# Transposed loads issued a stage earlier, and two elementwise passes moved to GpSimd with their neighbour sums moved to ScalarE

## The chip, the cores and the metric

The kernel runs on one core of one Trainium2 chip. The time is the device time of one execution in microseconds (us), given as the median over executions. Engines are named as in the profile: PE is TensorE, DVE is VectorE, ACT is ScalarE, POOL is GpSimd, SP is the engine whose queue issues nearly all DMAs here.

A ratio between two kernels is the mean time of one kernel's fast runs over the mean of the other's fast runs in the same rounds on the same chip, with a 95% interval. So it is not quite the ratio of the medians that stand beside it.

## The reference, cut to what matters

The forward pass is a modulated layer norm, a spectral mixing of the 2048 x 512 tokens (2-D FFT, product with complex weights, inverse FFT), a second modulated layer norm, and a two-layer network with squared ReLU. The kernel computes the output and the gradients of all nine differentiable inputs.

```python
x = A_x
mod = (silu(c) @ w_mod).reshape(1, 6, 1, 512)      # sa, ca, ga, sb, cb, gb
h = layernorm(x) * (1 + ca) + sa
x = x + ga * irfft2(rfft2(h) * (w_r + 1j * w_i))
h = layernorm(x) * (1 + cb) + sb
x = x + gb * (relu(h @ w1 + b1) ** 2 @ w2 + b2)
# reference: (x, *vjp(x wrt A_x, w_r, w_i, w1, b1, w2, b2, c, w_mod)(grad_out))
```

What this study touches is the last third of the backward pass:

- the **w1 stage**: the second spectral pass over eight groups of columns, which gives the gradients of w_r and w_i (tile gW), interleaved with the gradient of w1 (tile gw in its line 1085 before, 1086 after) and the gradient of w_mod (tiles wmc, gm_junk, gwm);
- the **short spectral stage** (tiles psG, utcs), whose first product marks the end of the w1 stage;
- the **last phase**: eight pairs of 128-row blocks go through the inverse transform and the backward of the first layer norm, while TensorE fills its time with the gradient of w2 (tile gw of line 1153 before, 1156 after). Column sums over the rows (tile acc) give two modulation gradients at the end.

## The kernel before

The loads of h for the w2 gradient are transposing DMAs of 512 KB into four rotating tiles. Before, the first four are issued behind the stage that needs the space, together with the first rows:

```python
    spec_f23(tc, K, UT, AEs, None, ..., ew_b, after_b)    # the w1 stage; after_b(gi) runs after each group
    lf2.release()
    gwp = tc.alloc_tile_pool(name="gwp", bufs=1, side="right")
    g_sb = gwp.tile([P, NT, D], BF16, name="g_sb")
    hns, endp = [], {}

    def load_hn():
        fc = len(hns)
        if fc < NFC:
            hns.append(endp.get("hn", gwp).tile([P, NT, P], BF16, name="hn", bufs=4))
            nc.sync.dma_start(hns[fc], h_dram[fc, :, :], transpose=True)
    # ... grad_w2, load_rows3 (two row loads per pair, n1 and gxl, from the same queue) cut ...
    nc.sync.dma_start(g_sb, g_view)
    load_hn()
    load_rows3(0)
    load_rows3(2)
    for _ in range(3):
        load_hn()
```

What runs after each group of the w1 stage, and two users of the same DMA queue in it:

```python
        def after_b(gi):
            if gi + 4 < 8:
                load(gi + 4)                  # Z, Xb and constants of a later group
            if gi == 4:
                nc.sync.dma_start(K["LG"], LG_dram)
            fill_w1(2 if 0 < gi < 6 else 1)   # w1 units: 16 matmuls, a copy on ScalarE, an output DMA
            if gi % 2 == 1:
                gms.pop(0)()                  # one w_mod gradient: GMod.emit
    # grad_w1: the output tile of two units
        if fb % 2 == 0:
            w1o[0] = gwa.tile([P, 2, W4], BF16, name="gw1", bufs=2)
        nc.scalar.copy(out=w1o[0][:, fb % 2, :], in_=ps[:, 0:W4])
        if fb % 2 == 1:
            nc.sync.dma_start(out4_view[...], w1o[0]...)
    # GMod.emit
            wmc = pool.tile([P, 2, D], BF16, name="wmc", bufs=self.bufs)      # bufs 2 here
            nc.sync.dma_start(wmc, self.wm_view[:, dc:dc + 2, cs])
            # ... on VectorE: sum of wmc * gmbc into junk ("gm_junk", line 465); gwm goes out by DMA ...
```

The row work of one pair in the last phase (gh1 is unfolded from gs by four 512-element passes on VectorE, lines 261 to 265):

```python
            nc.vector.tensor_tensor(gn, gh1, modb[...], op=ALU.mult)                                # line 1228
            for i in range(2):
                nc.scalar.activation(gs[:, i, :], gn[:, i, :], AF.Copy, scale=..., accum_out=rr[:, i, 0:1])
            nc.vector.tensor_tensor(q1, gh1, n1, op=ALU.mult)
            late.add(lambda: colsums1(t, gh1, q1))                                                  # TensorE
            for i in range(2):
                jk = fp.tile([P, D], BF16, name="jk1", bufs=1)
                nc.vector.scalar_tensor_tensor(out=jk, in0=gs[:, i, :], scalar=K["onef"], in1=n1[:, i, :], op0=ALU.mult, op1=ALU.mult,
                                               accum_out=rr[:, i, 1:2])
            nc.vector.tensor_scalar(rr[:, :, 2:4], rr[:, :, 0:2], -1.0 / D, None, op0=ALU.mult)
            for i in range(2):
                nc.vector.tensor_scalar(gn[:, i, :], n1[:, i, :], rr[:, i, 3:4], rr[:, i, 2:3], op0=ALU.mult, op1=ALU.add)
            nc.vector.tensor_tensor(gs, gn, gs, op=ALU.add)
            gx = fp.tile([P, 2, D], BF16, name="gx")
            nc.vector.tensor_tensor(gx, gs, gxl, op=ALU.add)
            nc.sync.dma_start(out1_view[:, t:t + 2, :], gx)
            load_rows3(t + 4)
```

## Time and profile before

| | us |
|---|---|
| median of 3 runs | 434.45 (434.1 to 438.83) |
| the profiled execution | 438.28, of which the trace covers 436.5 |
| first product of the short spectral stage (the w1 stage's end) | 340.8 |
| first and last pass q of the row chain | 362.9, 418.2 |
| last column sum | 419.1 |

The last three rows are starts in the trace, counted from its beginning. The profiled execution is the slow end of the three, so I use a second trace of the same kernel beside it (the last experiment), where the marks are 338.1, 359.9, 414.4, 415.3 and the end 432.7.

The stages and the waits of this trace stand in the prediction. Two lines more will be needed as a yardstick, the groups of two VectorE passes of the row chain between 345 and 437 us (after the bar: total busy us, mean ns of one; then the idle time before them):

```profile
L1228 DVE TENSOR_TENSOR gn<-gh,modb 128x1024 bf16<-128x1024 bf16 x8 | 5.5, 688 | 0.1
L1239 DVE TENSOR_SCALAR gn<-n,rr 128x512 bf16<-128x512 bf16 x16 | 5.8, 407 | 0.0
```

A pass over 1024 elements with two inputs takes 688 ns and one over 512 with per-partition scalars 407 ns, all of them nearly alike.

### The profile page before, as it was taken

To read this page: it belongs to the slowest core of one execution; us is meant where nothing else is said; L and a number is where in the kernel's file an instruction comes from. 1 tells how busy PE (TensorE), PEld (TensorE's weight loads), DVE (VectorE), ACT (ScalarE), POOL (GpSimd) and SP (SyncE) were. 2 spreads that over 40 slices of the span, in tenths; PEclk is the share of its full clock that TensorE was granted. 3 is DMA by queue.
4 is the path that set the end of the run, shared out by engine and by line. 5 is a ranking of instruction groups with operands and counts; after the bars stand their busy time and mean duration, and the time that the engine had idled before them with its cause. 6 is when DMAs were issued, how large, how long until landed. Compare 5 with 4: busy or idle time off the path is not lost.

```text
span 436.5 us, 7027 instructions
## 1 busy us (share of the span) xinstructions
PE 398.5 (91%) x2353; PEld 195.4 (45%) x2375; DVE 351.4 (80%) x846; ACT 261.2 (60%) x493; POOL 13.0 (3%) x64
## 2 busy tenths in 40 slices
PE   2789989999999999999999999999899799993996
PEld 0335446654444434443444444455455464441332
DVE  6887758959997588969897998909686968978896
ACT  5797889769881286348536765365348375445331
POOL 6120000000000000000000000000000000000000
PEclk9998999999999999999999999999999999999899
DMA  8995779999298469669965997987995699999984
GB/s 240 238 291 146 188 290 267 279 311 256 91 379 245 136 114 352 165 165 229 270 195 153 222 338 267 211 204 229 273 300 158 168 253 259 222 260 244 275 235 144
DMA packets 149738, 101.09 MB, mean 232 GB/s; under 512 B 98753, under 2 KB 135494, under 8 KB 149062
## 3 DMA queue, kind: packets, MB, share of 16 engines
q1 hardware_dynamic: 149138, 100.12, 86.6%
q10 hardware_dynamic: 564, 0.53, 0.4%
q8 instruction: 18, 0.29, 0.3%
q14 instruction: 18, 0.15, 0.1%
HBM read 35.44 MB, written 41.60 MB: 176 GB/s over the span
## 4 chain that ended last, share of the span: by engine, by line
PE 35%; DVE 28%; DMA 14%; ACT 12%; SPq 5%; issue 5%; POOL 1%; ACTq 0%; DVEq 0%
PE og L880 10%; PE mm L853 6%; PE mm L694 4%; PE mm L1150 4%; DMA n<-n_dram 3%; DMA out_dram<-gw 2%; DMA x<-in_A_x_dram 2%; DVE gm_junk L465 2%; PE psG L341 2%; SPq L1145 2%; PE mod_ps L595 2%; PE mm L1081 2%; DMA n_dram<-x_sb 2%; DVE l_st L795 1%; ACT r L855 1%
## 5 line engine op out<-in xcount | busy, mean ns | idle before, releaser
L694 PE MATMUL mm<-gT,w2T 128*128 128x512 bf16 x224 | 58.1, 383 | 3.4 <-DVE gab L697 2.7
L853 PE MATMUL mm<-h2T,w 128*128 128x512 bf16 x224 | 53.6, 379 | 1.7 <-ACT r L855 1.5
L1150 PE MATMUL mm<-g_sb,hn 128*128 128x512 bf16 x217 | 51.6, 387 | 3.8 <-DVE gw L1153 3.4
L1081 PE MATMUL mm<-gab,h_sb 128*128 128x448 bf16 x256 | 51.5, 352 | 2.5 <-ACT gw L1085 2.5
L880 PE MATMUL og<-w1T,gab 128*128 128x512 bf16 x218 | 49.9, 379 | 1.1 <-DVE o L945 0.8
L880 PE MATMUL og<-w,h 128*128 128x512 bf16 x217 | 49.1, 379 | 0.3
L855 ACT ACTIVATE r<-mm,b1col 128x512 bf16<-128x512 f32 x56 | 37.0, 684 | 6.1 <-PE mm L853 3.7
L1081 PEld LDWEIGHTS <-h_sb 128*128 128x128 bf16 x256 | 24.6, 98 | 24.2 <-issue 3.6
L853 PEld LDWEIGHTS <-w 128*128 128x128 bf16 x224 | 21.1, 97 | 30.6 <-issue 8.8
L1150 PEld LDWEIGHTS <-hn 128*128 128x128 bf16 x224 | 21.3, 99 | 29.8 <-issue 7.1
L880 PEld LDWEIGHTS <-h 128*128 128x128 bf16 x224 | 21.8, 98 | 26.1 <-issue 0.9
L880 PEld LDWEIGHTS <-gab 128*128 128x128 bf16 x224 | 21.6, 98 | 25.9 <-issue 1.4
L694 PEld LDWEIGHTS <-w2T 128*128 128x128 bf16 x224 | 20.9, 98 | 23.1 <-issue 6.5
L893 ACT CAST G<-og 128x512 bf16<-128x512 f32 x16 | 9.2, 580 | 27.9 <-PE og L880 27.9
L699 ACT CAST gab<-mm 128x512 bf16<-128x512 f32 x36 | 21.7, 602 | 3.0 <-PE mm L694 2.9
L857 DVE TENSOR_TENSOR h<-r 128x1024 bf16<-128x1024 bf16 x28 | 19.2, 687 | 4.8 <-ACT r L855 4.8
L1085 ACT CAST gw<-mm 128x448 bf16<-128x448 f32 x16 | 8.7, 543 | 24.0 <-DMA out_dram<-gw 15.0
L1230 ACT ACTIVATE gs<-gn,inv 128x512 bf16<-128x512 bf16 x16 | 11.4, 716 | 18.3 <-DVE gn L1228 18.3
L413 DVE TENSOR_TENSOR p<-Z,G 128x1028 bf16<-128x1028 bf16 x8 | 5.6, 697 | 19.9 <-DMA Xb<-xs_dram 11.6
L372 ACT ACTIVATE Tsb<-psT 128x512 bf16<-128x512 f32 x32 | 18.5, 604 | 1.6 <-PE psT L370 1.6
L465 DVE SCALAR_TENSOR_TENSOR gm_junk<-wmc,onef,gmbc 128x512 bf16<-128x512 bf16 x24 | 17.9, 747 | 1.9 <-DMA wmc<-in_w_mod_dram 1.0
L697 DVE CAST gab<-mm 128x512 bf16<-128x512 f32 x20 | 13.7, 686 | 6.8 <-PE mm L694 6.7
(287 smaller groups left out, 757.1 us busy)
## 6 DMA issues: line engine op xcount, KB each, us to landing
h_dram<-h SPq DMA_DIRECT2D x28, 256.0 KB, 3.6
gh_dram<-gab SPq DMA_DIRECT2D x28, 256.0 KB, 3.8
w<-in_B_w_dram SPq DMA_DIRECT2D x2, 1792.0 KB, 7.7
wmc<-in_w_mod_dram SPq DMA_DIRECT2D x12, 256.0 KB, 4.7
out_dram<-gwm SPq DMA_DIRECT2D x12, 256.0 KB, 3.7
wz_dram<-Z SPq DMA_DIRECT2D x8, 258.0 KB, 2.4
xs_dram<-Xs SPq DMA_DIRECT2D x8, 258.0 KB, 3.2
Z<-wz_dram SPq DMA_DIRECT2D x8, 258.0 KB, 4.3
```

Source lines behind the costliest of these rows:

```text
L372: nc.scalar.activation(Tsb, ps, AF.Copy, scale=EF_S)
L465: nc.vector.scalar_tensor_tensor(out=junk, in0=wmc[:, i, :], scalar=K["onef"], in1=gmbc, op0=ALU.mult, op1=ALU.mult, accum_out=self.gsc[:, ...
L694: nc.tensor.matmul(ps, lhsT=w2T[:, dc, fc * P:(fc + 1) * P], rhs=gT[b][:, :, dc, :], start=(dc == 0), stop=(dc == 3))
L697: nc.vector.tensor_copy(out=gaT[b][:, fc, :], in_=ps)
L699: nc.scalar.copy(out=gaT[b][:, fc, :], in_=ps)
L853: nc.tensor.matmul(ps, lhsT=w1[:, dc, (fc + i) * P:(fc + i + 1) * P], rhs=h2T[b][:, :, dc, :], start=(dc == 0), stop=(dc == 3))
L855: nc.scalar.activation(r[:, i, :], ps, AF.Relu, bias=b1col[:, fc + i:fc + i + 1])
L857: nc.vector.tensor_tensor(h2, r, r, op=ALU.mult)
L880: nc.tensor.matmul(ps, lhsT=lhs(fc), rhs=rhs[:, fc, :], start=(fc == 0), stop=(fc == NFC - 1))
L1081: nc.tensor.matmul(ps[:, 0:W4], lhsT=h2_sb[:, t, dc * P:(dc + 1) * P], rhs=ghn[t // 4][:, t % 4, fs], start=(t == 0), stop=(t == NT - 1))
L1150: nc.tensor.matmul(ps, lhsT=hns[fc][:, t, :], rhs=g_sb[:, t, :], start=(t == 0), stop=(t == NT - 1))
L1230: nc.scalar.activation(gs[:, i, :], gn[:, i, :], AF.Copy, scale=inv1[:, t + i:t + i + 1], accum_out=rr[:, i, 0:1])
```

## The change

Its intent: the transposed loads should leave the crowded start of the last phase, and VectorE should lose four of its costliest passes per pair to engines that have time, GpSimd (q and gx) and ScalarE (the running sums, with a new product on VectorE in front of them).

```diff
+    hnp = tc.alloc_tile_pool(name="hnp", bufs=1, side="right")      # ahead of the w1 stage
+    hns, endp = [], {}
+    def load_hn(): ...                                              # as before, with hnp in place of gwp
@@ after_b(gi)
                 nc.sync.dma_start(K["LG"], LG_dram)
+            if 1 <= gi < 5:
+                load_hn()
             fill_w1(2 if 0 < gi < 6 else 1)
@@
     nc.sync.dma_start(g_sb, g_view)
-    load_hn()
     load_rows3(0)
     load_rows3(2)
-    for _ in range(3):
-        load_hn()
@@ row_pair
-            nc.vector.tensor_tensor(q1, gh1, n1, op=ALU.mult)
+            nc.gpsimd.tensor_tensor(q1, gh1, n1, op=ALU.mult)
             late.add(lambda: colsums1(t, gh1, q1))
+            nc.vector.tensor_tensor(gn, gs, n1, op=ALU.mult)
             for i in range(2):
-                jk = ...; nc.vector.scalar_tensor_tensor(out=jk, ..., accum_out=rr[:, i, 1:2])
+                nc.scalar.activation(gn[:, i, :], gn[:, i, :], AF.Copy, accum_out=rr[:, i, 1:2])
@@
-            nc.vector.tensor_tensor(gx, gs, gxl, op=ALU.add)
+            nc.gpsimd.tensor_tensor(gx, gs, gxl, op=ALU.add)
```

I call the first half part 1 and the edits in row_pair part 2.

More of the change, by code (lines that the diff above doesn't have):

```diff
@@ L1087, in grad_w1, with load_hn @@
             nc.sync.dma_start(out4_view[:, dc, (fb - 1) * W4:(fb + 1) * W4], w1o[0].rearrange("p a f -> p (a f)"))
+    hns, endp = [], {}
+    def load_hn():
+        fc = len(hns)
+        if fc < NFC:
+            hns.append(endp.get("hn", hnp).tile([P, NT, P], BF16, name="hn", bufs=4))
+            nc.sync.dma_start(hns[fc], h_dram[fc, :, :], transpose=True)
     units = []
@@ L1137 @@
     g_sb = gwp.tile([P, NT, D], BF16, name="g_sb")
-    hns, endp = [], {}
-    def load_hn():
-        fc = len(hns)
-        if fc < NFC:
-            hns.append(endp.get("hn", gwp).tile([P, NT, P], BF16, name="hn", bufs=4))
-            nc.sync.dma_start(hns[fc], h_dram[fc, :, :], transpose=True)
     def grad_w2(fc):
@@ L1230, in row_pair @@
                 nc.scalar.activation(gs[:, i, :], gn[:, i, :], AF.Copy, scale=inv1[:, t + i:t + i + 1], accum_out=rr[:, i, 0:1])
-            nc.vector.tensor_tensor(q1, gh1, n1, op=ALU.mult)
+            nc.gpsimd.tensor_tensor(q1, gh1, n1, op=ALU.mult)
             late.add(lambda: colsums1(t, gh1, q1))
+            nc.vector.tensor_tensor(gn, gs, n1, op=ALU.mult)
             for i in range(2):
-                jk = fp.tile([P, D], BF16, name="jk1", bufs=1)
-                nc.vector.scalar_tensor_tensor(out=jk, in0=gs[:, i, :], scalar=K["onef"], in1=n1[:, i, :], op0=ALU.mult, op1=ALU.mult,
-                                               accum_out=rr[:, i, 1:2])
+                nc.scalar.activation(gn[:, i, :], gn[:, i, :], AF.Copy, accum_out=rr[:, i, 1:2])
             nc.vector.tensor_scalar(rr[:, :, 2:4], rr[:, :, 0:2], -1.0 / D, None, op0=ALU.mult)
@@ L1284 @@
     gwp.release()
+    hnp.release()
     h2p.release()
```

## The prediction

> **What bounds the kernel now.** I began with the page's table of busy time and then asked for the busy time of each engine by stage, because a share over the whole span mixes stages. The change only touches what happens after about 300 us: the second spectral pass with the w1 gradient (about 286 to 341 us), the short spectral stage after it (341 to 356), and the last phase, in which pairs of rows go through VectorE and ScalarE while TensorE works off the w2 gradient (356 to the end).
>
> ```profile
> PE 398.5 (91%) x2353; PEld 195.4 (45%) x2375; DVE 351.4 (80%) x846; ACT 261.2 (60%) x493; POOL 13.0 (3%) x64
> ```
> ```profile
> core 0: us, PE busy (x) PEld busy (x) DVE busy (x) ACT busy (x) POOL busy (x), PEclk, DMA share, GB/s
> 303.00:323.00 20.00, 18.28 (x115) 10.22 (x113) 14.73 (x38) 8.65 (x17) 0.00 (x0) 1.00 0.93 264
> 323.00:341.00 18.00, 17.19 (x111) 9.81 (x110) 13.85 (x32) 9.46 (x18) 0.00 (x0) 1.00 0.68 206
> 341.00:356.00 15.00, 12.60 (x120) 8.83 (x119) 14.52 (x35) 7.97 (x15) 0.00 (x0) 1.00 0.67 212
> 356.00:394.00 38.00, 37.48 (x232) 17.96 (x235) 29.44 (x71) 19.58 (x45) 0.00 (x0) 1.00 1.08 245
> 394.00:404.00 10.00, 3.12 (x21) 1.10 (x19) 8.62 (x21) 5.74 (x13) 0.00 (x0) 0.96 1.06 230
> 404.00:421.00 17.00, 16.89 (x76) 6.43 (x77) 15.73 (x39) 5.53 (x13) 0.00 (x0) 0.92 1.00 257
> 421.00:433.00 12.00, 11.45 (x51) 4.63 (x50) 10.87 (x31) 3.84 (x6) 0.00 (x0) 1.00 0.70 217
> ```
>
> Read the PE column against the length of each stretch. TensorE is full nearly everywhere; what it loses is 1.72 + 0.81 us in the w1 gradient, 2.4 us in 341 to 356, 0.52 us, then 6.88 us in one hole from 394 to 404, then 0.11 and 0.55. The last column but one says that the DMA engines are full from 356 to 421. VectorE is busy but not full in any stretch except 341 to 356. So I asked for the chain of work around the hole, and for the DMA queue in the same time.
>
> ```profile
> 388.23 0.45 DVE gw L1153
> 388.68 3.98 DMA n<-n_dram
> ...
> 395.17 0.68 DVE gw L1153
> ...
> 397.83 3.95 DMA n<-n_dram
> 401.84 0.57 issue
> 402.41 0.70 DVE gw L1153
> 403.11 0.04 issue
> 403.15 1.86 PE mm L1150 x4
> ```
> ```profile
> 383.73 4.86 SPq L1145 DMA_TRANSPOSE hn<-h_dram  x2
> 388.68 0.53 SPq L1170 DMA_DIRECT2D n<-n_dram  x1
> ...
> 393.27 4.46 SPq L1145 DMA_TRANSPOSE hn<-h_dram  x1
> 397.83 0.52 SPq L1170 DMA_DIRECT2D n<-n_dram  x1
> ```
>
> The hole is a chain of four: a transposed load of h occupies the one DMA queue for 4 to 5 us; the row load n behind it is issued late and lands 4 us later; VectorE, which works in order, stands at its product q with n (the waits give 6.2 us in 3 waits for it, the first one at 362.9 us); and behind that product stands the eviction gw, which TensorE needs in order to reuse one of two PSUM tiles. Two such waits make the hole of 6.88 us. The bound of the last phase is thus the DMA queue, through VectorE's order, and TensorE's own work right behind it.
>
> **What the Trainium skill says.** "GPSIMD Engine Reference", section 3.1: a two-input elementwise pass costs about 2.6 cycles an element at 1.2 GHz, and VectorE is about twice as fast in fp32. The trace before has no pass of that size on GpSimd (its only tensor_tensor are 128x4 and took 1064 ns), so it neither agrees nor disagrees. "SBUF — State Buffer", section Who interferes with whom: a VectorE instruction with two SBUF inputs contends with a GpSimd instruction that reads SBUF, and the second one to issue can be blocked until the first is done. No stretch of this trace has both, so nothing shows it. "ScalarE: Activation LUTs", rules for kernel authors: about 0.3 us for an ACTIVATE and 0.83 ns an element, so 0.72 us for 512; the trace agrees (716 ns for the scaled copy with a sum, and 189 ns for reading the sum out). "DMA: Bandwidth & Descriptors", Latency and other measured facts: 261 GB/s for a transposing DMA, which makes 2.0 us for a tile of 512 KB; here the 14 loads of h held the queue for 3.1 us at the median (1.9 to 7.2), and landed in 5.6 us, so this case is slower, and I use its own number.
>
> **Part 1, the four early loads.** Four of the 14 transposed loads (2 MB) leave the stretch 351 to 370 us, where they take 7.23 us (the first, just behind the 2 MB load of the output gradient) and 8.52 us (the next three) of the queue, 15.7 us together. They come after groups 1 to 4 of the spectral pass, which I place at about 303 to 325 us. What this saves: the first n lands at 362.9 now, 11.6 us after the queue began the first transpose; without that transpose n is behind the gradient alone, so I expect it at about 358 to 360, and the first wait of 1.7 us disappears. The output and row loads from 361 on no longer stand behind 8.5 us of transposes. And the DMA engines, full for 58 us (14.7 MB between 351 and 409 us, 254 GB/s), have 2 MB less to move: 8.3 us at that rate, more than the 6.2 us that VectorE waits for n. I take it that the hole of 6.9 us closes: minus 6.9 us. More than that is not to be had, as TensorE is otherwise full from 356 on.
>
> What it costs: the w1 gradient stage. There the queue already works almost without a pause from 299 to 331 us, the DMA share is 0.93 from 303 to 323, and TensorE's 2.53 us of idle time come from one thing:
>
> ```profile
> ACT gw L1085 <- DMA out_dram<-gw: 15.0, 2, 8.0
> ```
>
> ScalarE cannot evict a w1 tile until the output of an older one has left, since there are two output tiles. Four more transposes of 3.1 us put 12.5 us into the queue in front of these outputs. Some of it is hidden: the queue waits for VectorE's gW for 6.8 us in that stage, TensorE has a lag of two tiles, and from 331 to 341 the queue has air. By estimate each of the two waits grows by a little over 1 us, plus 2.5 us in all, with 0 and 6 us as the bounds I can argue for.
>
> **Part 2, work taken from VectorE.** Start to start, a pass of 1024 elements with two inputs takes 0.60 us on VectorE in the timeline, one of 512 in the unfolding 0.34, one with a per-partition scalar 0.33, and the multiply with a running sum 0.67 and 0.08 for the read-out.
>
> ```profile
> L1235 DVE SCALAR_TENSOR_TENSOR jk<-gs,onef,n 128x512 bf16<-128x512 bf16 x16 | 12.0, 747 | 0.7 <-ACT gs L1230 0.3
> L1231 DVE TENSOR_TENSOR q<-gh,n 128x1024 bf16<-128x1024 bf16 x8 | 5.5, 687 | 6.2 <-DMA n<-n_dram 6.2
> L1242 DVE TENSOR_TENSOR gx<-gs,gxl 128x1024 bf16<-128x1024 bf16 x8 | 5.5, 683 | 0.0
> ```
>
> Each of the eight pairs of rows loses q (0.60), two sums (1.50) and gx (0.60) on VectorE and gains one product (0.60): minus 2.1 us a pair, minus 16.8 us over the phase. ScalarE gains two copies with a sum, 0.72 us each start to start, so 1.44 us a pair and 11.5 us in all; it is busy for about half of the phase now and stays under TensorE. GpSimd gets two passes of 1024 elements a pair: 1024 x 2.6 / 1.2 GHz = 2.2 us each by the skill's figure, 35 us over eight pairs, an estimate.
>
> What of this lies on the path: pairs of rows follow each other at 7.9 us now (q of the first pair at 362.94, of the last at 418.18, seven intervals), of which VectorE works about 7. The last pair's column sum releases the two modulation gradients, and from there to the end are some 17 us. TensorE's w2 gradient ends at the same time, 432.5 us. So a faster row chain alone cannot move the end, and a much slower one would.
>
> **The rivals.** First, the port: what VectorE keeps of a pair is nearly all with two SBUF inputs or in a fast mode: 4 x 0.34 + 3 x 0.60 + 2 x 0.33 = 3.8 us. If GpSimd and VectorE exclude each other wholly, a pair needs 3.8 + 4.4 = 8.2 us in place of 7.9, the saving of 16.8 us is paid back, and the row chain ends at about 360 + 7 x 8.2 = 418, as late as now. Then nothing comes from part 1 either, the cost in the w1 stage stays, and the time is 436 to 440. For it: the skill's rule. Against it: nothing in the trace; and GpSimd has more than half of the time free, so that part can fall beside evictions from PSUM. If both share the port by access, a pair takes about 7 us and the chain ends at about 410: then TensorE alone bounds the end. Second, the latency: the ring of two gs tiles already makes ScalarE wait for gx (12.3 us in 3 waits, the longest 5.4). The loop grows by ScalarE's sums and by GpSimd's 2.2 us in place of 0.60, from about 9 to 11 or 13 us for two pairs in flight, 5.5 to 6.5 us a pair; still under 7.9, so it is not the bound, but it uses up most of what VectorE gave. Third, the early loads may be hidden wholly in the w1 stage (the queue has waits of its own): then the time falls by 7 to 8 us, to 427. Fourth, they may make TensorE wait for both output tiles at each of the four loads: plus 6 us, and the time stays at 434.
>
> **Range and chances.** 434.45 - 6.9 (the hole) + 2.5 (the w1 stage) + 0.5 (the row chain's own spill under contention) = 430.5 us. The best case is TensorE's own floor: all of its idle time after 356, 6.88 + 0.52 + 0.11 + 0.55 = 8.1 us, gone at no cost, 426.4, which is still short of 2% (425.8). Only a gain in 341 to 356 as well, or in the w1 stage, would pass it. The worst that I can argue, the port exclusive and the w1 stage 6 us longer, is 440 to 445. So the range is 424.5 to 440, and the chances are 0.16 for faster by over 2%, 0.73 for within 2%, 0.11 for slower.
>
> **What would show it.** Right: TensorE's idle time between 356 and 433 falls from 8.1 us to 2 or less; VectorE no longer waits for n; the idle time of ScalarE for w1 outputs grows from 15 us; in the w1 stage TensorE loses some 5 us in place of 2.5; GpSimd's passes take 2.2 us or more, and VectorE's two-input passes become longer than 687 ns on average. Wrong: if a hole as long as the old one stands later in the last phase, with waits for GpSimd or ScalarE's sum (the ring or the port is the bound); if the passes on GpSimd last 4 us, so that it becomes the slowest engine of the row chain; or if the w1 stage ends as early as before (the early loads are free).

## The result, and the profile after

| | before | after |
|---|---|---|
| median us | 435.54 of 4 runs (434.1 to 438.83) | 461.10 of 4 runs (460.68 to 462.53) |
| ratio of the fast runs | | 1.0581 (95%: 1.0512 to 1.0651) |
| traced span | 436.5 | 459.0 |
| first product of the short stage | 340.8 | 354.9 |
| first and last q | 362.9, 418.2 | 375.1, 432.4 |
| last column sum | 419.1 | 434.9 |

The changed kernel is 5.8% slower and computes the same, correct outputs. The marks say at once that there are two losses: 14.1 us until the short stage starts, and a row chain that is no faster and leaves 24.1 us of work after its last column sum, where 17.4 were left before.

First the same stretches as in the prediction, for the kernel after (columns: stretch and its length, busy us and number of instructions of PE, PEld, DVE, ACT, POOL, the granted TensorE clock, the DMA engines' busy share, GB/s):

```profile
303.00:323.00 20.00, 16.08 (x92) 8.60 (x91) 10.63 (x26) 6.55 (x13) 0.00 (x0) 0.91 0.94 236
323.00:341.00 18.00, 15.56 (x99) 8.82 (x98) 10.95 (x26) 5.15 (x11) 0.00 (x0) 1.00 0.64 203
341.00:356.00 15.00, 8.11 (x35) 4.26 (x35) 7.10 (x18) 6.78 (x13) 0.00 (x0) 0.66 0.74 200
394.00:404.00 10.00, 6.21 (x30) 2.84 (x31) 7.75 (x13) 7.84 (x20) 5.72 (x3) 0.83 0.57 171
404.00:421.00 17.00, 12.51 (x77) 5.12 (x77) 15.57 (x24) 8.30 (x20) 9.44 (x5) 0.92 0.78 186
```

In the first two stretches TensorE now idles 3.9 and 2.4 us where it lost 1.7 and 0.8, and in the third, which is still the w1 stage here, 6.9 of 15 us. It also does less in its busy time: 92 products in 16.08 us against 115 in 18.28, at a granted clock of 0.91. The DMA engines have a third of their time free in the second of them and a quarter in the third (0.64 and 0.74), so throughput is not what all three engines lack there; something makes everybody wait in turn. In the last two stretches the old hole has company: TensorE idles 3.8 and 4.5 us, with the DMA engines at 0.57 and 0.78.

**The w1 stage.** The DMA queue, then the three engines at the worst place, from the timelines of the kernel after (start us, duration, and in brackets how long the engine stood before it and for what):

```profile
335.61 2.50 SPq L1132 DMA_DIRECT2D out_dram<-gW  x4
338.15 3.31 SPq L1096 DMA_TRANSPOSE hn<-h_dram  x1
341.57 0.52 SPq L1088 DMA_DIRECT2D out_dram<-gw  x1
...
345.41 0.44 SPq L458 DMA_DIRECT2D wmc<-in_w_mod_dram  x1
```
```profile
344.43 0.53 ACT L1086 CAST gw<-mm 128x448 bf16<-128x448 f32 x1 [9.13 <-DMA out_dram<-gw]
```
```profile
347.89 1.88 PE L306 MATMUL psC<-AE,LFb 128*128 128x257 bf16 x8 [9.33 <-ACT G L308]
```
```profile
348.90 0.75 DVE L465 SCALAR_TENSOR_TENSOR gm_junk<-wmc,onef,gmbc 128x512 bf16<-128x512 bf16 x1 [8.69 <-DMA wmc<-in_w_mod_dram]
```

Read it as a ring. Between 328.65 and 335.61 the queue issues nothing: its next entry is the output of gW, which VectorE has not made, because VectorE stood for 5.2 us at the product gm_junk, until the wmc tile had come at 330.57, and does the products of gm_junk before those of gW. Then come the gW outputs (2.5 us), a transposed load (3.3 us), and only then the w1 output for which ScalarE has stood 9.1 us, and the wmc tile for which VectorE has stood 8.7 us again. TensorE stands 9.3 us because the copies of G are behind ScalarE's blocked eviction. Before, the waits for wmc were 1.0 us in all and those for w1 outputs 15.0 us; after, they are 13.9 and 28.4.

**The last phase.** The groups of VectorE from 340 us to the end, then of GpSimd, in the kernel after:

```profile
L1238 DVE TENSOR_SCALAR gn<-n,rr 128x512 bf16<-128x512 bf16 x16 | 9.5, 633 | 0.2
...
L1228 DVE TENSOR_TENSOR gn<-gh,modb 128x1024 bf16<-128x1024 bf16 x8 | 9.0, 1129 | 0.1
L1156 DVE TENSOR_TENSOR gw<-mm,modb 128x512 bf16<-128x512 f32 x14 | 9.6, 683 | 2.3 <-PE mm L1153 2.3
```
```profile
L1231 POOL TENSOR_TENSOR q<-gh,n 128x1024 bf16<-128x1024 bf16 x8 | 19.7, 2458 | 133.3 <-PE psT L370 123.0 <-DVE gh L265 4.6 <-DVE rr L1236 2.5
L1241 POOL TENSOR_TENSOR gx<-gs,gxl 128x1024 bf16<-128x1024 bf16 x8 | 18.1, 2259 | 21.1 <-DVE gs L1239 19.0 <-issue 2.1
```

The two yardstick groups went from 407 to 633 ns and from 688 to 1129 ns, while the eviction gw, with one input in PSUM and one in SBUF, stays at 683. On the page, VectorE's busy time rose from 351.4 to 357.7 us, although the change took 16.8 us of passes from it by the prediction's count. A mean of 1129 ns hides what happens; a single place in the two timelines shows it:

```profile
378.95 0.68 DVE L1233 TENSOR_TENSOR gn<-gs,n 128x1024 bf16<-128x1024 bf16 x1
379.56 2.61 DVE L1228 TENSOR_TENSOR gn<-gh,modb 128x1024 bf16<-128x1024 bf16 x1
382.19 0.69 DVE L1156 TENSOR_TENSOR gw<-mm,modb 128x512 bf16<-128x512 f32 x1
```
```profile
379.17 2.45 POOL L1231 TENSOR_TENSOR q<-gh,n 128x1024 bf16<-128x1024 bf16 x1 [1.54 <-DVE gh L265]
```

The product that began before q takes its usual 0.68 us. The next one starts 0.4 us into q and lasts until 382.17: q's end (381.62) plus 0.55 us. It stood still for as long as GpSimd ran. Behind it, in order, stands gw, which TensorE needs. That gw itself is not held is visible at 392.95 us, where one takes 0.68 us in the midst of a q that runs from 392.39 to 395.0:

```profile
392.95 0.68 DVE L1156 TENSOR_TENSOR gw<-mm,modb 128x512 bf16<-128x512 f32 x1
```

### The profile page after: what moved, and what is told of

Same layout as the page of the kernel before. It is cut to its first block, busy times and chain, and to the rows that moved or that the text cites. A ratio compares the mean times of both kernels' runs of the same rounds, so it can differ in the third digit from the quotient of the medians.

```text
span 459.0 us, 7066 instructions
## 1 busy us (share of the span) xinstructions
PE 405.7 (88%) x2353; PEld 197.7 (43%) x2375; DVE 357.7 (78%) x806; ACT 271.8 (59%) x525; POOL 50.7 (11%) x80
## 5 line engine op out<-in xcount | busy, mean ns | idle before, releaser
L1082 PE MATMUL mm<-gab,h_sb 128*128 128x448 bf16 x256 | 55.0, 370 | 3.9 <-ACT gw L1086 3.9
L1082 PEld LDWEIGHTS <-h_sb 128*128 128x128 bf16 x256 | 25.7, 102 | 28.2 <-issue 9.3
L1231 POOL TENSOR_TENSOR q<-gh,n 128x1024 bf16<-128x1024 bf16 x8 | 19.7, 2458 | 133.3 <-PE psT L370 123.0
L853 PEld LDWEIGHTS <-w 128*128 128x128 bf16 x224 | 21.1, 97 | 30.6 <-issue 8.8
L1086 ACT CAST gw<-mm 128x448 bf16<-128x448 f32 x16 | 8.8, 549 | 40.7 <-DMA out_dram<-gw 28.4
L880 PEld LDWEIGHTS <-gab 128*128 128x128 bf16 x224 | 21.6, 98 | 25.9 <-issue 1.4
L465 DVE SCALAR_TENSOR_TENSOR gm_junk<-wmc,onef,gmbc 128x512 bf16<-128x512 bf16 x24 | 19.7, 822 | 14.7 <-DMA wmc<-in_w_mod_dram 13.9
L1241 POOL TENSOR_TENSOR gx<-gs,gxl 128x1024 bf16<-128x1024 bf16 x8 | 18.1, 2259 | 21.1 <-DVE gs L1239 19.0
```

Source lines behind the costliest of these rows:

```text
L465: nc.vector.scalar_tensor_tensor(out=junk, in0=wmc[:, i, :], scalar=K["onef"], in1=gmbc, op0=ALU.mult, op1=ALU.mult, accum_out=self.gsc[:, ...
L853: nc.tensor.matmul(ps, lhsT=w1[:, dc, (fc + i) * P:(fc + i + 1) * P], rhs=h2T[b][:, :, dc, :], start=(dc == 0), stop=(dc == 3))
L880: nc.tensor.matmul(ps, lhsT=lhs(fc), rhs=rhs[:, fc, :], start=(fc == 0), stop=(fc == NFC - 1))
L1082: nc.tensor.matmul(ps[:, 0:W4], lhsT=h2_sb[:, t, dc * P:(dc + 1) * P], rhs=ghn[t // 4][:, t % 4, fs], start=(t == 0), stop=(t == NT - 1))
L1231: nc.gpsimd.tensor_tensor(q1, gh1, n1, op=ALU.mult)
L1241: nc.gpsimd.tensor_tensor(gx, gs, gxl, op=ALU.add)
```

## The experiments

All outputs were correct. The question after the result was: which part costs what, and by which mechanism? For part 2 the theory is the exclusive hold of what GpSimd and VectorE share; the rival is the longer chain of dependences through ScalarE and GpSimd. For part 1 the theory is the order of the one DMA queue; the rivals are the time of the four transposes themselves and the two output tiles alone.

### The parts alone

`loads_only` is part 1 without part 2; `rows_only` is part 2 without part 1. `acts_only` and `pool_only` split part 2:

```diff
 acts_only, against before: only the sums
-   jk = ...; nc.vector.scalar_tensor_tensor(out=jk, ..., accum_out=rr[:, i, 1:2])
+   nc.vector.tensor_tensor(gn, gs, n1, op=ALU.mult)
+   nc.scalar.activation(gn[:, i, :], gn[:, i, :], AF.Copy, accum_out=rr[:, i, 1:2])
 pool_only, against before: only the engine of q and gx
-   nc.vector.tensor_tensor(q1, ...); nc.vector.tensor_tensor(gx, ...)
+   nc.gpsimd.tensor_tensor(q1, ...); nc.gpsimd.tensor_tensor(gx, ...)
```

> Part 1 alone: the four transposed loads of h go out in the w1-gradient stage, the row passes stay as before. Theory A (two separate losses; this one is a ring of in-order queues in the w1 stage): the first matmul of the short spectral stage comes 10 to 15 us later than the 340.8 us of before, ScalarE waits 25 us or more for w1 outputs, and the last phase gets 5 to 8 us shorter as its hole closes; 438 to 445 us. Rival B (all of the loss is GpSimd's passes, and the later start of the short stage is a side effect of their place in the schedule): 427 to 432 us.

> Part 2 alone: GpSimd's two passes and ScalarE's sums, with the loads of h where before has them. Theory A: the w1 stage is as before (short spectral stage from about 341 us), the last phase is 8 to 15 us longer, VectorE instructions that fall under a GpSimd pass last up to 2.6 us; 443 to 450 us. Rival B (the early loads are the whole loss): 431 to 437 us.

> Only the running sums go to ScalarE (one product on VectorE, two copies with a sum on ScalarE); nothing on GpSimd, no early loads. If the shared port is what costs in part 2: no VectorE instruction is stretched, VectorE has about 6 us less to do, and the time is 430 to 436 us. If the longer chain through ScalarE (two more hops a pair) is what costs: 440 us or more, with VectorE waiting for the sums.

> Only q and gx go to GpSimd; the sums stay on VectorE, the loads are where before has them. If the shared port is what costs: 8 to 16 us lost, 443 to 452 us, with VectorE's two-input passes stretched by 15 us or more in total, as the multiply with a sum has two inputs in SBUF too. If the port costs little: VectorE has 9.6 us less and the time is 430 to 436 us.

| | median us | ratio (95%) | short stage starts | first q | last q | last column sum | end of trace |
|---|---|---|---|---|---|---|---|
| before (first trace) | 435.72 in these rounds | | 340.8 | 362.9 | 418.2 | 419.1 | 436.5 |
| before (second trace) | | | 338.1 | 359.9 | 414.4 | 415.3 | 432.7 |
| loads_only | 444.26 | 1.0217 (1.0157 to 1.0277) | 355.2 | 376.0 | 424.5 | 425.5 | 443.1 |
| rows_only | 453.07 | 1.0418 (1.0358 to 1.0478) | 339.7 | 361.6 | 424.0 | 426.7 | 451.1 |
| acts_only | 434.27 | 0.9998 (0.9937 to 1.0058) | 337.9 | 359.4 | 411.4 | 412.4 | 432.7 |
| pool_only | 451.44 | 1.0385 (1.0311 to 1.0459) | 338.9 | 360.7 | 424.3 | 426.9 | 449.5 |
| after | 461.10 | 1.0581 (1.0512 to 1.0651) | 354.9 | 375.1 | 432.4 | 434.9 | 459.0 |

By medians part 1 costs 8.5 us and part 2 17.35, in sum 25.9; both together cost 25.6. The parts add up, so each can be explained alone.

Part 1: the w1 stage ends at 355.2, some 14 us later than in the first trace of before and 17 later than in the second. From there to the end it takes 87.9 us in place of 95.7 or 94.6. So the last phase does gain 7 to 8 us, and the w1 stage eats it twice.

Part 2, rows_only against the second trace of before: the first q is 1.7 us later, the eight pairs take 62.4 us in place of 54.5 (+7.9), the last column sum comes 2.7 us after the last q in place of 0.9 (+1.8), and 24.4 us of work are left after it in place of 17.4 (+7.0). The sum is 18.4, the difference of the two spans. The last term is w2 gradient that TensorE could not do earlier: it works in order, with row products between, and idles 17.9 us from 356 to 433 where before idled 8.1 and 10.5 in its two traces. Its own pace is a part of the loss too: from the last product of the short stage to the end, the same 387 products keep it busy for 76.8 us at a granted clock of 0.91, against 71.3 us at 0.97 in the second trace of before. That is 5.5 us more of work, beside 11.2 us more of idle time. No run parts the lower clock from the idle time; GpSimd's being busy is not enough for it, as pool_memset below has 0.98 in the same stretch. The loss is larger than I expected: 453.07 us against 443 to 450.

acts_only shortens the eight pairs to 52.0 us, but 20.3 us are left after the last column sum, and the time is the same to 0.1%: a faster row chain alone doesn't move the end. It also excludes ScalarE's sums by themselves as a cause. pool_only, which has GpSimd's two passes alone, has 15.7 of the 17.35 us: nearly the whole loss of part 2 sits in these passes.

### What GpSimd's passes hold up

`rows_split` is rows_only with each GpSimd pass cut into two of 512 elements. `q_only` is acts_only with q on GpSimd and gx left on VectorE. `pool_memset` is acts_only with eight memsets per pair on GpSimd, which write SBUF and read nothing:

```diff
 rows_split, against rows_only (gx likewise)
-   nc.gpsimd.tensor_tensor(q1, gh1, n1, op=ALU.mult)
+   for i in range(2):
+       nc.gpsimd.tensor_tensor(q1[:, i, :], gh1[:, i, :], n1[:, i, :], op=ALU.mult)
 q_only, against acts_only
-   nc.vector.tensor_tensor(q1, gh1, n1, op=ALU.mult)
+   nc.gpsimd.tensor_tensor(q1, gh1, n1, op=ALU.mult)
 pool_memset, against acts_only, behind q
+   pj = fp.tile([P, D], BF16, name="pj", bufs=1)
+   for _ in range(8):
+       nc.gpsimd.memset(pj, 0.0)
```

> Part 2 alone, with each of GpSimd's passes of 1024 elements cut into two of 512. If the port is held for one whole GpSimd instruction at a time: a VectorE instruction under it waits 1.2 to 1.4 us at most in place of 2.0, but GpSimd's total is as long or longer, so the stretch of VectorE in total stays at 12 to 20 us and the time at 447 to 456 us. If VectorE is only slowed in proportion while GpSimd runs: its longest instructions stay as long as in the run of part 2 alone.

> ScalarE's sums, and of the two passes only q on GpSimd; gx stays on VectorE, the loads are where before has them. If each GpSimd pass costs what it holds VectorE up: about half of the 17.5 us of part 2, 441 to 446 us, with 8 to 11 us of stretch on VectorE. If gx on GpSimd is what costs, since it ends the ring of gs tiles: 433 to 438 us.

> The row passes with ScalarE's sums and everything else on VectorE, and beside them eight writes of zeros of 512 elements a pair on GpSimd, which read nothing from SBUF. If it is GpSimd's reading that holds VectorE's two-input passes: they keep their 685 ns, only the 512-element passes with a per-partition scalar may be stretched, and the time is 433 to 438 us. If any GpSimd work holds VectorE: two-input passes are stretched as in part 2 and the time is 440 us or more.

pool_memset took 435.02 us, ratio 1.0009 (0.9955 to 1.0064). Its groups on VectorE and GpSimd:

```profile
L1231 DVE TENSOR_TENSOR q<-gh,n 128x1024 bf16<-128x1024 bf16 x8 | 5.5, 687 | 2.0 <-DMA n<-n_dram 2.0
```
```profile
L1234 POOL MEMSET pj<- 128x512 bf16 x64 | 33.8, 528 | 102.5 <-PE psG L341 98.8
```

GpSimd is busy for 33.8 us, about as long as with its two passes (36.4 in rows_only), and no pass with two inputs grows. Only the passes with per-partition scalars (409 ns in acts_only) rose to 488, which the time doesn't show. So it isn't GpSimd's being busy, nor its writing, that holds VectorE's two-input passes. What the memsets leave out is the reading.

q_only took 445.12 us, ratio 1.0232 (1.0184 to 1.028), 10.9 us over acts_only. Half of the GpSimd passes, 19.3 us of them, stretch VectorE's passes by 11.2 us in all: lines 1228, 1233 and 261 have means of 1142, 1168 and 900 ns in place of 689, 685 and 419. That's more than the 4.8 us of q that VectorE lost.

rows_split took 447.17 us, ratio 1.0297 (1.0243 to 1.0351), 5 to 6 us better than rows_only (by the ratios or by the medians), though GpSimd's busy time rose from 36.4 to 43 us. The product of gs and n took up to 2.61 us in rows_only; the longest of them under half a pass is this one:

```profile
373.20 1.64 DVE L1234 TENSOR_TENSOR gn<-gs,n 128x1024 bf16<-128x1024 bf16 x1
```

The hold lasts for one GpSimd instruction. Shorter ones hold for a shorter time, and VectorE gets in between them. The rival, a longer chain of dependences, asks for the opposite: the two halves of a pass take longer together than the whole, so with them the chain is longer, and the time should have risen.

### Where the early loads cost

Three of these are part 1 without part 2, with one thing changed; the first has the new pool, with the loads written where before has them:

```diff
 own_pool_late, against loads_only: the new pool, the loads written where before has them
-            if 1 <= gi < 5:
-                load_hn()
     nc.sync.dma_start(g_sb, g_view)
+    load_hn()
     load_rows3(0)
     load_rows3(2)
+    for _ in range(3):
+        load_hn()
 loads_behind: load_hn() behind gms.pop(0)() in after_b
 loads_at4:    if gi >= 4: load_hn()
 loads_gw4:    four w1 output tiles in a pool that has room during the stage, two afterwards
+            early = len(units) > 4
+            w1o[0] = (w1o["pool"] if early else gwa).tile(..., name="gw1", bufs=4 if early else 2)
```

> A control for the early loads: the four tiles of h in the same separate pool as in the change, but loaded where before loads them. If the early transposes make the loss: as before, 433 to 438 us, with the short spectral stage from about 341 us and the hole in the last phase back. If the other place in memory and the order of the queue that follows from it make the loss: 441 to 446 us.

> The early loads alone, with four tiles in place of two for w1 outputs during the w1 stage. If what costs there is ScalarE standing at an eviction of a w1 tile until the output of an older one has left the one queue (and TensorE, the G copies and VectorE behind ScalarE): these waits fall from 28 us to under 5, the short spectral stage begins at 342 to 347 us in place of 355.2, the gain in the last phase stays, and the time is 428 to 436 us. If what costs is the queue's and the DMA engines' time for the transposes themselves, or VectorE's wait for the w_mod loads: the stage begins no earlier than 352 us and the time stays at 441 to 445 us.

> The four early loads again, but each is written behind the modulation gradient of its group in place of ahead of it; in the queue's order, which the build fixes, the second pair of w_mod loads then stands ahead of the third transpose and not behind it. If the loss of 14 us in the w1 stage comes from the order in the one queue (w_mod loads late, VectorE standing for them in front of the gW products, whose outputs are in front of the next w_mod loads): the short spectral stage begins at 341 to 347 us in place of 355.2, VectorE waits under 6 us for w_mod in that stage in place of 14, and the time is 428 to 436 us. If the transposes cost by their own time, wherever they stand: still 352 us or later, and 441 to 445 us.

> The four early loads behind groups 4 to 7 of the spectral pass in place of 1 to 4, where the queue had air in the kernel before. The build still puts two of them ahead of the stage; of the other two, both stand behind the first four w_mod loads. If the order in the queue is what costs: the short spectral stage begins at 341 to 347 us, 428 to 436 us. If the transposes' own time costs: 438 to 445 us.

| | median us | ratio (95%) | third and fourth load issued | short stage, first to last product | VectorE's waits for wmc | ScalarE's for w1 outputs |
|---|---|---|---|---|---|---|
| before | 434.67 / 434.85 in these rounds | | after the stage | 340.8 to 353.4 / 338.1 to 350.7 | 1.0 / 1.2 | 15.0 / 12.3 |
| own_pool_late | 437.16 | 1.0067 (1.0016 to 1.0118) | 336.6, 344.7 | 344.7 to 361.8 | 10.6 | 16.1 |
| loads_only | 444.26 | 1.0217 (1.0157 to 1.0277) | 317.1, 338.8 | 355.2 to 368.2 | 14.2 | 28.2 |
| loads_behind | 440.91 | 1.0149 (1.01 to 1.0199) | 324.8, 334.6 | 347.1 to 362.8 | 10.6 | 15.6 |
| loads_at4 | 436.91 | 1.0055 (1.0013 to 1.0097) | 334.7, 341.5 | 342.4 to 358.6 | 6.3 | 20.1 |
| loads_gw4 | 446.33 | 1.0276 (1.0233 to 1.0318) | 319.3, 339.2 | 346.4 to 369.4 | 21.1 | 0 |

(The waits are counted within the w1 stage and the start of the short one; loads_only is from the rounds above, with before at 435.72.) In all five changed kernels the first two loads leave at 282 to 289 us, so only the third and the fourth have another place.

own_pool_late is not the control that it was meant to be. The build fixes the order of the queue, and with tiles of their own the loads did not wait for the stage to end. Its trace has all four ahead of the short stage or at its start; these are the last two:

```profile
336.58 3.59 SPq L1096 DMA_TRANSPOSE hn<-h_dram  x1
...
344.74 3.18 SPq L1096 DMA_TRANSPOSE hn<-h_dram  x1
```

So it is one more order of the queue, and no run shows what the new pool costs by itself.

The clearest pair of lines is the short stage in loads_only and in loads_at4 (count, then minimum, median and maximum ns, then the first and last start):

```profile
L341 PE MATMUL psG<-LGb,Z x64: 269/272/287, 355.2 to 368.2; 128*128 128x256 bf16 x64
```
```profile
L341 PE MATMUL psG<-LGb,Z x64: 269/273/421, 342.4 to 358.6; 128*128 128x256 bf16 x64
```

The same four transposes move the start by 12.8 us and the end by 9.6 us (the short stage takes 3.2 us longer in loads_at4, where TensorE stands 4.5 us in it for a copy on ScalarE, against 0.2), by nothing but their place in the queue. So most of the delay is the place, and the first rival, their own 12 to 16 us of queue time, falls as the whole cost. A part of it may stay: even in loads_at4 the short stage ends 5.2 to 7.9 us later than in before, and no run says how much of that is the loads' own time. loads_behind, with the same groups but behind the w_mod loads, lies between the two. Both took longer than I expected (428 to 436 us), and in loads_behind the waits for wmc fell to 10.6 us only, not under 6.

loads_gw4 was meant to show that two output tiles are the whole cost. Its short stage starts early, as expected, but ends last of all (369.4), and the time was missed: with four tiles ScalarE never waits for a w1 output, and VectorE's waits become longer instead.

```profile
DVE gm_junk L465 <- DMA wmc<-in_w_mod_dram: 21.1, 2, 12.6
```

The queue has two branches to a waiting engine here, and cutting one leaves the other. That suggested the next kernel, loads_gw4 with the wmc loads from GpSimd's queue as well:

```diff
 loads_gw4_wmpool, against loads_gw4
-            nc.sync.dma_start(wmc, self.wm_view[:, dc:dc + 2, cs])
+            nc.gpsimd.dma_start(wmc, self.wm_view[:, dc:dc + 2, cs])
```

> The early loads as in the change, with four tiles for w1 outputs and with the w_mod loads issued from GpSimd's own queue, so that neither ScalarE nor VectorE depends on a transfer that stands behind the transposes. If the ring through the one queue is the loss, both of its branches are cut: the stage begins at 340 to 346 us, 427 to 434 us. If not, it begins at 350 us or later and the time is 440 us or more. The two ways of cutting it are tried together because more w1 tiles alone moved the wait to the w_mod loads.

It took 439.25 us, ratio 1.0112 (1.007 to 1.0153). The half about the stage came true: TensorE is busy for 38.00 of the 38 us from 303 to 341, and the short stage starts at 344.9. So the two waits together can account for TensorE's stops. It is not a pure test, since the build moved the loads again: three of them leave at 282 to 292 us, and the fourth at 330.3. The half about the time was missed: the short stage takes 3.6 us longer (344.9 to 361.1, in before 340.8 to 353.4), and the whole is 4.4 us slower than before.

### Is the hole of the last phase worth anything?

In all these versions the wait for the row load n is gone. From the last product of the short stage to the end it takes 74.9 us in loads_only, 75.0 in loads_behind, 75.9 in loads_at4, 75.8 in own_pool_late, 75.0 in loads_gw4 and 76.3 in loads_gw4_wmpool, against 83.1 and 82.0 in the two traces of before. So the last phase gains what I had hoped, own_pool_late's too, since its loads had left the phase as well. But what comes before it grew each time by more, measured against the second trace of before. To see whether the hole can be closed without moving the transposes, the row loads alone went to another queue, which leaves the order of TensorE, VectorE and ScalarE as in before:

```diff
 rows_queue, against before; acts_rows_queue: the same against acts_only
-            nc.sync.dma_start(rows3[t][0], n1_dram[:, t:t + 2, :])
-            nc.sync.dma_start(rows3[t][1], gx1_dram[:, t:t + 2, :])
+            nc.gpsimd.dma_start(rows3[t][0], n1_dram[:, t:t + 2, :])
+            nc.gpsimd.dma_start(rows3[t][1], gx1_dram[:, t:t + 2, :])
```

> The kernel before, with one thing changed: the loads of the rows n and gxl in the last phase are issued from GpSimd's own queue, so that they do not stand behind the transposed loads of h; TensorE, VectorE and ScalarE have the same instructions in the same order as before. If the hole from 394 to 404 us comes from the place of n in the one queue, as the prediction has it: VectorE's waits for n fall from 6.2 us to under 2, TensorE's hole from 6.9 to under 3, and the time falls by 3 to 7 us, 428 to 432. If the DMA engines themselves are the limit, n comes as late as before and the time stays at 433 to 437 us.

> The same, with the running sums on ScalarE as in the change (6 us less on VectorE). If the place of n in the queue is what the last phase waits for, VectorE's lighter load can pay only now: 425 to 431 us. If the running sums are worth nothing with n on time either: as the run with the row loads alone.

> The kernel before, unchanged, for a second trace: the first one is of an execution of 438.3 us, 3 to 4 us above the median. If the hole from 394 to 404 us and the waits for n belong to the kernel, they stand in this trace too, at about the same place; the span is 431 to 434 us if the execution takes the median time.

| | median us | ratio (95%) |
|---|---|---|
| before | 434.18 of 11 | |
| before_again (one look) | 434.54 | |
| rows_queue | 439.63 of 6 (433.66 to 442.75) | 1.0066 (1.0008 to 1.0124) |
| acts_rows_queue | 438.65 of 6 | 1.0098 (1.0059 to 1.0138) |

(Two of the six runs of rows_queue count as slow and are not in the ratio; the other four are 433.66 to 440.07.) In rows_queue the wait for n fell from 6.2 to 0.4 us, as the theory said. The idle time did not go: from 356 to 404 TensorE stands for 6.2 us (4.3 up to 394 and 1.9 after), against 7.4 and 6.3 in the two traces of before. (The traced execution is the one of 439.2 us, from the slow half of the four; the one of 433.66 us has no trace.) The second stretch and one of the new waits:

```profile
394.00:404.00 10.00, 8.07 (x30) 3.02 (x31) 9.14 (x22) 2.54 (x5) 2.11 (x4) 0.66 1.12 263
```
```profile
DVE gx L1242 <- DMA out_dram<-gx: 4.1, 1, 4.1
```

VectorE now stands for outputs that have not left (gx 4.1 us, gw 3.6), at a DMA share of 1.12, and TensorE's granted clock in this stretch is 0.66. A reading that fits, and that no run tests by itself: the transfers of the last phase compete for the DMA engines, and if the row loads come earlier, outputs leave later. acts_rows_queue, expected at 425 to 431 us, gained no more. before_again shows the hole in a second execution of the unchanged kernel (TensorE is busy for 6.03 of 10 us in 394 to 404), so it belongs to the kernel; it is not a matter of one slow trace.

No version here is faster than before; acts_only and pool_memset tie with it.

## Why the prediction was wrong

The prediction was 434.45 - 6.9 + 2.5 + 0.5 = 430.5 us, and the range ended at 440 (the worst case that it argued itself, 440 to 445, lay above that). The kernel took 461.1. Term by term:

- **"the hole", -6.9.** Right in size for the phase: loads_only gains 6.7 to 7.8 us from the short stage on, and no wait for n is left. As to the cause it was half right. The transposes do hold n back in the queue, but rows_queue puts n on time by itself and gains nothing. What every version with a shorter phase has in common is that 2 MB left it, and they had to go somewhere.
- **"the w1 stage", +2.5, with 6 us as the bound.** Mis-sized: it measured +14 to +17 us. The prediction looked at one wait, ScalarE's for w1 outputs, and let it grow by a little over 1 us twice; it grew by 13 us. It left out the second branch, VectorE's for wmc, since that cost 1.0 us in the trace before. And it added queue time to waits as if they lay in a line, where the trace after has a ring: queue, VectorE's product, gW, queue again. It also placed all four loads at 303 to 325 us; in the trace they are issued at 282.4, 287.2, 316.2 and 338.2, and the last one sits in the middle of the longest stop.
- **"the row chain's own spill under contention", +0.5.** This is the step that failed by most: it measured +17 us. The rival named it rightly, even the pair time: "a pair needs 3.8 + 4.4 = 8.2 us", and the trace after has (432.4 - 375.1) / 7 = 8.2. That the number agrees so well is partly luck: rows_only, without the early loads, has (424.0 - 361.6) / 7 = 8.9. Nor was GpSimd free for "more than half of the time" among the pairs, as the prediction had it: 4.4 of 7.9 us a pair is more than half busy, and the evictions that its passes should fall beside are 9.6 us in all, 1.2 us a pair. What I had against it, that GpSimd's passes could fall beside PSUM evictions, is true of the single instruction (gw runs 0.68 us beside q) and useless for the engine: VectorE issues in order, and the next pass that is held is rarely far behind, so q and gx hold the evictions that come after it too.
- **What an exclusive port makes of the time, "436 to 440".** Too small even under the right rival. It took the row chain's end as the end of the damage. But TensorE works in order through row products and w2 products, so whatever delays the chain also keeps w2 work for after it: 24.1 us are left after the last column sum where 17.4 were left before. Of the 18.4 us between rows_only and the second trace of before, 7.0 are that.
- **The passes' cost on GpSimd, 2.2 us by estimate.** Right: 2.26 and 2.46 us.
- **The latency of the ring through ScalarE and GpSimd.** Not the bound, as argued; acts_only has ScalarE's part of it and loses nothing.
- **"a faster row chain alone cannot move the end".** Right: acts_only shortens the pairs by 2.5 us and has 2.9 us more left behind them.

What stays open: how the loss of the last phase in rows_queue divides between the shared DMA engines, the order of the outputs and TensorE's clock; what the new pool costs by itself; and how much of the w1 stage's delay is the loads' own time.

## What to carry to other kernels

Before work goes to GpSimd, count what VectorE still does beside it: in this kernel a GpSimd pass that reads SBUF stopped VectorE's next two-input pass until it ended (2.61 us in place of 0.69), passes with per-partition scalars grew as well (407 to 633 ns), and everything in order behind them waited, so a pass moved off VectorE can cost it more than it took. Before a load is moved forward in a queue that several engines wait on, list every later entry of that queue and who stands for it; the place among those entries can matter more than the load's own time. Look the order up in the trace, and not in the program: own_pool_late was written with late loads and ran with early ones. And check what a freed wait exposes: here a hole of 7 us in a phase whose DMA engines are full was closed, in every version that moved the loads, at the price of a longer phase before it.

## What the Trainium skill lacked or had wrong

- "SBUF — State Buffer", section Who interferes with whom: right in both halves that matter here. The second to issue stood until the first was done (a VectorE product took 2.61 us in place of 0.69 under a GpSimd pass of 2.45 us), and GpSimd writes alone left two-input passes at 687 ns. What it does not draw is the consequence of VectorE's order: passes that don't contend, such as evictions from PSUM (0.68 us each throughout), wait behind one that does, so 16 GpSimd passes of 36 us in all cost 17 us end to end.
- "GPSIMD Engine Reference", section 3.1: the 2.6 cycles an element held in bf16 as well (1024 elements took 2.26 to 2.46 us, or 2.6 to 2.9 cycles at the page's 1.2 GHz). Its ratio to VectorE, about 2 in fp32, did not carry over: VectorE's bf16 pass takes 0.69 us, a ratio of 3.3 to 3.6.
- "DMA: Bandwidth & Descriptors", Latency and other measured facts: 261 GB/s for a transposing load would be 2.0 us for 512 KB, by estimate. Here such a load landed 5.6 us after its issue at the median, among other traffic. It also held the issuing queue, and everything behind it, for 3.1 us at the median (1.9 to 7.2); for a load of this size the page gives no such time.
- The same page, Issuing engines are not separate DMA queues: agrees in the outcome, as with row loads from a second queue the kernel was no faster (ratio 1.0066). The issue time that this saves, which the page calls usually small, was not small here: the loads came on time, and 6.2 us of waits became 0.4.
- No page tells that one in-order queue with in-order engines can close to a ring; four loads at different places in the queue gave 436.9, 437.2, 440.9 and 444.3 us.
